# Blocked attention with a mixture of experts behind it: blank rows move to GpSimd's queue, the last batch's router tiles get a home of their own, and eight hand-written orders of steps are dealt anew

## The chip, the cores and the metric

The kernel runs on one core of a Trainium2 chip. TensorE (PE) multiplies, VectorE (DVE) and ScalarE (ACT) work elementwise, GpSimd (POOL) adds, computes powers and issues some DMAs, and SyncE (SP) issues the other loads. Each engine takes its instructions in the order in which they were written, and waits on semaphores for what other engines and DMAs owe it. The metric is the device time of one execution in microseconds (us), lower is better.

## The reference, cut to what matters

```python
# attention: 8 batches, 8 heads, 576 positions, 64 features, block-causal mask of 64
scores = np.where(mask, scale * q @ k.T, -1e9)
attn = np.exp(scores - scores.max(-1)); attn /= attn.sum(-1) + 1e-9
x = (attn @ v) with the heads side by side            # 4608 rows of 512
# router: cosine similarity to 8 experts, softmax, the best one alone
xn, en = x / (norm(x) + 1e-6), emb / (norm(emb) + 1e-6)
logits = xn @ en.T / tau
idx, gate_w = argmax(logits), softmax(logits)[idx]
# each row goes through its own expert: 512 -> 1024 -> 512
out[rows of e] = gate_w * (relu(x[rows of e] @ w1[e]) @ w2[e])
```

## The kernel before, in words

**Two halves.** The first half is attention and routing: 32 pairs of heads, numbered 0 to 31, four for each of the eight batches. The second half runs the experts over slots of 128 rows. Between them lies a handover, in which the last batch is routed while the first expert's weights are split and two early slots are worked.

**A pair in attention.** Instructions are written by a loop over the pairs (line 659). Each pair advances several generators, one step for each letter of a string in `PLANS` (line 22). `PLANS[0]` to `PLANS[3]` serve the four pairs of a batch, `PLANS[4]` to `PLANS[7]` those of pairs 28 to 31, and pair 0 has `PLAN0`. The letters are:

- `s`: the scores of pair n in five chunks. Each chunk is matmuls on PE into a two-bank PSUM buffer (`psp`, three of them) and an exponential on ACT into `pT`. After the third, the fourth and the fifth, POOL adds parts of `pT` into `pS` (line 347). These additions are called add 1 (after the third chunk), add 2 (the fourth), adds 3 and 4 (the fifth).
- `v`: the values of pair n-1 into the one PSUM tile `psb`. The first six steps are matmuls with V, the seventh the sums over keys (lines 392 to 397), which read `pT` and the finished `pS`, the eighth the copy `so` on ACT (line 399), the ninth is empty.
- `f`: finishing pair n-1. Two steps of small matmuls that read `so` and write `psb` again, then DVE's division into the row buffer (`xrow` or `xodd`, line 428), then the logits `lgh` (line 431).
- `m`: the row maxima of pair n+1, four steps of PE into `psp` and DVE out of it, one for the diagonal, one that transposes them.
- `p`: preparing pair n+2: transposes on PE into `psp`, `hi` on ACT, `lo` on DVE, two times.
- `l` and `w`: loads on SP's queue for pair n+3.
- `r`: one step of the router for the batch that ended before (`route`, from line 447).

What a pair has not done when its string ends is done at once.

**The router's steps.** The last pair of a batch is finished in the first pair of the next batch, and the router of the batch starts in the pair after that: its four router pairs are those numbered 4b+5 to 4b+8. It has 42 steps: 1 to 7 find the best expert on DVE, 8 ranks the rows with six small matmuls on PE, 9 and 10 add up the counts, 12 to 16 are five squares on ACT, 17 a power on POOL, 18 to 20 the places of the rows, 21 to 27 the gate (24 an exponential on ACT, 23 a product on DVE). Steps 30, 33, 36, 39 and 42 are `rows_out` (line 546), an indirect DMA issued by POOL that sends 128 rows to their places in the array `xs` in DRAM. They are called OUT 0 to OUT 4. For the seventh batch there are four more steps behind step 11, the squares are 16 to 20, the power 21, and the OUTs 32 to 36 follow without gaps; then two early slots are read back from `xs` (line 570).

In the strings before, the order of the other letters is the same in all eight. The `r` stand between them as follows, for a batch's four router pairs: steps 1 and 2, steps 3 to 13, steps 14 to 40, steps 41 and 42. In the third, OUT 0 stands before the third chunk of scores, OUT 1 between the third and the fourth, OUT 2 between the fourth and the fifth, OUT 3 behind it. For the seventh batch steps 1 to 31 are in pair 29, the five OUTs at the head of pair 30.

**Blank rows.** `blank(e)` (line 553) writes 128 rows of zeros (twice for expert 0) into `xs`, where an expert's first slot may read rows that nobody sends. It runs at the head of pairs 1, 2 and 3, for experts 0 to 2, 3 to 5, 6 and 7, and its nine DMAs are issued by SP.

**The handover's memory.** Attention's buffers lie in pools stacked from the right end of the memory: `st` outermost, then `xlast` (holding `xodd`), `xpool`, `rt`, `sm` (the router's small tiles, two of each, and a scratch) and `ptp`. When the chain of the last batch's routing is written, these pools but `st` are given up, and `ring(1)` puts the second layer's split weights over them: `ring_h1`, 32 KB in each partition, and `ring_l1`, 32 KB. A new tile waits for all instructions and DMAs that still use an old tile under it. The first to write is ACT (line 711, called by `seconds_in`, line 1123), and the piece stands ahead of the second half of `h` for early slot b (line 1094) in ACT's queue.

Of the kernel before, what the change touches and what calls it, by code (L numbers as in the profile page):

```python
# [8 lines left out]
F32 = mybir.dt.float32  # L9
F32R = mybir.dt.float32r  # L10
BF16 = mybir.dt.bfloat16
I32 = mybir.dt.int32
# [6 lines left out]


PLANS = (
    "vrvrrmrrmrmrrvrrvrrvrvrrvrrlrrvrsrrsrrprrmrfrrprrmrsrrfrrwrrvrsrrprrfrrsrfrrprrmrr",
    "vvmmmvvvvvlvssprmfpmsfwvspfsfpmr",
    "vvmrmmvrvvvrvlrvssrpmfrpmsrfwrvsprfsfrpmr",
    "vvrmrmrmrvrvrvrvrvrlvrsrsrprmrfrprmrsrfwrvrsrprfrsrfrprmr",
    "vrvrrmrmrrmrrvrvrrvrvrrvrrlrvrrsrsrrprrmrfrrprmrrsrrfrwrrvrsrrprrfrsrrfrprrmrr",
    "vrvrmrmrmrvrvrvrvrvrlrvrsrsrprmrfrprmrsrfrwrvrsrprfrsrfrprmrr",
    "vvrmrmrmvrvrvrvvrlrvrssrprmrfrpmrsrfrwvrsrprfsrfrprmr",
    "vrvrmrrmrmrvrrvrvrvrrvrlrrvrsrsrrprmrfrrprmrsrrfrwrrvrsrprrfrsrfrrprmrr",
)  # L30
PLAN0 = "mksmsmskmpkppmslpswp"

# [2 lines left out]
def kernel(  # L35
# [12 lines left out]
    nc = tc.nc  # L48
    B, H, S, D = q.shape
    E, DM, DF = w1.shape  # L50
    NT = B * S
    P = 128
    NP = H // 2
    NJ = (S - 64) // P + 1
# [17 lines left out]
    xs = dram.tile([E * RE * P, RW], F32, name="xs")  # L72
# [27 lines left out]
    ebase = iota("ebase", [P, NJ, E], [[0, NJ], [RE * P, E]])  # L100
# [54 lines left out]
    sm = pool(right, "sm", 2, side="right")  # L155
# [11 lines left out]
    def one_bank():  # L167
        return two_banks()[:, 0]
# [275 lines left out]
    def bc(ap, *shape):  # L444
        return ap.to_broadcast(shape)

    def route(b, xrow, lgh, ssp):

        lg = sm.tile([P, NJ, E], F32, name="lg")
        mx = sm.tile([P, NJ], F32, name="mx")  # L450
        t1 = sm.tile([P, NJ, E], F32, name="t1")
        ohb = sm.tile([P, NJ, E], BF16, name="ohb")
        nc.vector.tensor_reduce(lg, lgh.rearrange("p j h e -> p j e h"), axis=AX.X, op=ALU.add)
        yield
        nc.vector.tensor_reduce(mx, lg, axis=AX.X, op=ALU.max)
        yield
        nc.vector.tensor_tensor(lg, lg, bc(mx.unsqueeze(2), P, NJ, E), op=ALU.subtract)
        yield

        nc.vector.scalar_tensor_tensor(t1, lg, 0.0, erev, op0=ALU.is_ge, op1=ALU.mult)  # L460
        yield
        nc.vector.tensor_reduce(mx, t1, axis=AX.X, op=ALU.max)
        yield
        nc.vector.tensor_tensor(ohb, t1, bc(mx.unsqueeze(2), P, NJ, E), op=ALU.is_equal)
        yield
        nc.vector.memset(ohb[0:64, 0, :], 0.0)
        yield

        rk_ps = one_bank() if b < B - 1 else ps_m.tile([P, 512], F32, name="psm")
        rk = rk_ps[:, 0:NJ * E].rearrange("p (j e) -> p j e", e=E)  # L470
        yield "pe"
        nc.tensor.matmul(rk, triS, ohb, start=True, stop=False)
        for j in range(NJ - 1):
            nj = NJ - 1 - j
            nc.tensor.matmul(rk[:, j + 1:NJ, :], onesb, bc(ohb[:, j:j + 1, :], P, nj, E), start=False, stop=False)
        nc.tensor.matmul(rk, onesb, bc(acc.unsqueeze(1), P, NJ, E), start=False, stop=True)
        if b < B - 1:
            t2 = above(rk, ebase)
        else:
            ends.append((rk, ohb))  # L480
        yield
        oa = sm.tile([P, E], F32, name="oa")
        nc.vector.tensor_reduce(oa, ohb.rearrange("p j e -> p e j"), axis=AX.X, op=ALU.add)
        yield
        nc.vector.tensor_tensor(acc, acc, oa, op=ALU.add)
        yield
        if b == B - 1:
            nc.vector.tensor_tensor(accb, acc, early, op=ALU.subtract)
        yield "counted"
        if b == B - 2:  # L490

            c0 = one_bank()[:, 0:1]
            nc.tensor.matmul(c0, onesb, acc[:, 0:1], start=True, stop=True)
            lack = sm.tile([P, 1], F32, name="lack")
            yield
            nc.vector.scalar_tensor_tensor(lack, c0, -1.0, lim, op0=ALU.mult, op1=ALU.add)
            yield
            nc.vector.tensor_scalar(lack, lack, 0.0, float(EARLY), op0=ALU.max, op1=ALU.min)
            yield
            nc.vector.tensor_tensor(acc[:, 0:1], acc[:, 0:1], lack, op=ALU.add)  # L500
            yield

        ss = sm.tile([P, NJ], F32, name="ss")
        gs = sm.tile([P, NJ], F32, name="gs")
        if b < B - 1:
            for j in range(NJ):
                squares(xrow[:, j, 0:DM], ss[:, j:j + 1])
                yield
        else:
            nc.vector.tensor_reduce(ss, ssp, axis=AX.X, op=ALU.add)  # L510
        nc.gpsimd.tensor_tensor(ss, ss, half, op=ALU.pow)
        yield
        if b < B - 1:
            rowj = yield from places(t2, ohb)
        nc.vector.tensor_scalar(ss, ss, 1.0e-6, None, op0=ALU.add)
        yield
        nc.vector.reciprocal(ss, ss)
        yield
        nc.vector.tensor_tensor(lg, lg, bc(ss.unsqueeze(2), P, NJ, E), op=ALU.mult)
        yield  # L520
        nc.scalar.activation(lg, lg, AF.Exp)
        yield
        nc.vector.tensor_reduce(gs, lg, axis=AX.X, op=ALU.add)
        yield
        nc.vector.tensor_scalar(gs, gs, 1.0e-9, None, op0=ALU.add)
        yield
        if b == B - 1:
# [25 lines left out]
    def blank(e):  # L553

        t = ex[0]
        if e == 0:
            nc.gpsimd.memset(t, 0.0)
            nc.gpsimd.memset(t[:, DM + 1:DM + 2].bitcast(I32), 1 << 30)
        for r in range(EARLY if e == 0 else 1):
            r0 = (e * RE + r) * P  # L560
            nc.sync.dma_start(xs[r0:r0 + P, :], t)

    def token(tail):
        return tail[:, 1:2].bitcast(I32)
# [5 lines left out]
            nc.gpsimd.dma_start(ex[u], xs[u * P:(u + 1) * P, :])  # L570
            yield

    def above(rk, base):
        t = sm.tile([P, NJ, E], F32, name="t2")
        nc.vector.tensor_tensor(t, rk, base, op=ALU.add)
        return t

    def places(t, ohb):

        row = sm.tile([P, NJ], F32, name="row")  # L580
        rowj = sm.tile([P, NJ], I32, name="rowj")
        nc.vector.tensor_tensor(t, t, ohb, op=ALU.mult)
        yield
        nc.vector.tensor_reduce(row, t, axis=AX.X, op=ALU.add)
        yield
        nc.vector.tensor_tensor(rowj, row, drop, op=ALU.add)
        yield
        return rowj
# [70 lines left out]
    for n in range(NPAIR):  # L659
        pTs = pTf[n % 2]  # L660
        parts = {"s": scores(n, pTs), "v": pv, "f": post(n - 1) if n >= 1 else None,
                 "m": maxes(n + 1) if n + 1 < NPAIR else None,
                 "p": prep(n + 2) if n + 2 < NPAIR else None}
        for e in range(3 * n - 3, min(3 * n, E)) if n else ():
            blank(e)
        for c in PLANS[n % NP + (NP if n >= NPAIR - NP else 0)] if n else PLAN0:
            if c == "w":
                if n + 3 < NPAIR:
                    load_v(n + 3)
            elif c == "l":  # L670
# [326 lines left out]
    def chain():  # L997
# [13 lines left out]
            yield c  # L1011

        rk, ohb = ends[0]
        pg = places(above(rk, ebase), ohb)
        next(pg)
        next(rg)
        next(pg)
# [2 lines left out]
        rowj = finished(pg)  # L1020
# [17 lines left out]
    mx = ctx.enter_context(tc.tile_pool(name="mx", bufs=1, reuse_waits="tile"))  # L1038
# [64 lines left out]
    a, b = ea  # L1103
# [190 lines left out]
```

## Time and profile before

| what | value |
|---|---|
| median of 3 runs | 878.1 us (876.48 to 878.93) |
| the profiled execution | 880.13 us |
| its span, first to last instruction | 878.5 us |
| PE busy | 813.9 us, 93% |
| DVE busy | 530.1 us, 60% |
| POOL busy | 415.6 us, 47% |
| ACT busy | 404.6 us, 46% |
| mean granted clock of TensorE | 0.972 of full speed |

The profiled execution lies 2.0 us over the median, and 1.6 us of it lie around its span. Busy time of PE is modelled and matmuls overlap, so 93% says that PE is nearly always at work, and the idle rest is what a change of order can win. In the rows below a pair is cut from one copy `so` to the next, so that a stretch holds the second half of one string and the first of the next.

### The profile page before, as it was taken

The page shows a single profiled execution, that of the slowest core. Times are in us where ns is not written, and L with a number is a line of the kernel's source. Part 1 is how long each engine was busy: PE and PEld are TensorE (multiplying, and loading weights), DVE is VectorE, ACT ScalarE, POOL GpSimd, SP SyncE. Part 2 cuts the span into 40 slices and gives each one's busy share as a digit, 9 for nine tenths or more (in the row PEclk, how much of TensorE's full clock was granted, in tenths as well). Part 3 has the DMA queues.
Part 4 walks back from the last instruction along what each step waited for, and adds up shares of the span by engine and source line. Part 5 has one row for each costly group of instructions (what it writes and reads, how often), then busy time and mean ns, then how long its engine had stood idle before and what let it go on. Part 6 is the DMA issues. An engine that isn't in the chain of part 4 may idle for free. (4 is left out here: it accounts for less than half of the span.)

```text
span 878.5 us, 21354 instructions
## 1 busy us (share of the span) xinstructions
PE 813.9 (93%) x6569; PEld 643.9 (73%) x6569; DVE 530.1 (60%) x992; ACT 404.6 (46%) x733; POOL 415.6 (47%) x547
## 2 busy tenths in 40 slices
PE   6899989898999989858969999999999999999996
PEld 3677767676767767646657888888888888888875
DVE  5667767676775767652855534655767444666441
ACT  2344635545464546443634444654555333444321
POOL 4344564647464565644241133324455646465551
PEclk9899999999998999978989999999999999999998
DMA  4864444545345444507355453566687545354441
GB/s 72 185 148 83 74 109 82 138 83 122 79 91 109 84 118 73 126 1 244 125 198 196 159 167 96 175 213 220 219 259 230 183 137 160 108 182 156 137 134 40
DMA packets 147525, 121.17 MB, mean 138 GB/s; under 512 B 122991, under 2 KB 123311, under 8 KB 145837
## 3 DMA queue, kind: packets, MB, share of 16 engines
q1 hardware_dynamic: 123760, 64.50, 30.5%
q0 software_dynamic: 16976, 42.81, 16.4%
q10 hardware_dynamic: 6636, 12.09, 3.8%
q8 instruction: 63, 1.03, 0.5%
q14 instruction: 90, 0.73, 0.3%
HBM read 84.90 MB, written 35.27 MB: 137 GB/s over the span
## 5 line engine op out<-in xcount | busy, mean ns | idle before, releaser
L316 DVE TENSOR_REDUCE nmx<-psp 128x2 f32<-128x1024 f32 (+3 forms) x128 | 103.3, 824 | 85.3 <-PE psp L235 84.1
L365 ACT ACTIVATE pT<-psp 128x576 f32<-128x576 f32 (+2 forms) x192 | 112.4, 618 | 65.2 <-PE psp L235 51.1
L347 POOL TENSOR_TENSOR pS<-pT 128x896 f32<-128x896 f32 (+1 forms) x32 | 66.2, 2069 | 156.6 <-ACT pT L365 156.6
L235 PE MATMUL psp<-hi 64*128 64x448 f32 (+6 forms) x768 | 123.7, 354 | 9.0 <-ACT pT L365 4.0
L933 PE MATMUL py<-ring_h,hh 128*128 (+1 forms) x288 | 112.7, 391 | 0.5 <-issue 0.5
L933 PE MATMUL py<-ring_h,hl 128*128 (+1 forms) x288 | 112.2, 390 | 0.0
L933 PE MATMUL py<-ring_l,hh 128*128 (+1 forms) x288 | 112.1, 389 | 0.0
L933 PE MATMUL ph<-ring_h,xh 128*128 x280 | 110.1, 393 | 0.3 <-issue 0.3
L235 PEld LDWEIGHTS psp<-hi 64*128 64x128 f32 (+1 forms) x768 | 73.3, 190 | 48.9 <-DVE lo L301 16.0
L933 PE MATMUL ph<-ring_h,xl 128*128 x280 | 109.1, 389 | 0.0
L933 PE MATMUL ph<-ring_l,xh 128*128 x280 | 109.0, 389 | 0.0
L383 PE MATMUL psb<-pT,vo 128*64 128x448 f32 (+4 forms) x768 | 101.9, 401 | 6.6 <-DVE lgh L431 5.4
L347 POOL TENSOR_TENSOR pS<-pS,pT 128x640 f32<-128x640 f32 (+3 forms) x96 | 95.4, 994 | 8.0 <-ACT pT L365 1.4
L891 POOL DMA_DIRECT2D hq<-hrows x92 | 50.3, 553 | 101.1 <-DVE px L861 85.0
L715 DVE TENSOR_TENSOR ring_l<-raw,ring_h 128x1024 f32 (+1 forms) x64 | 77.6, 1224 | 22.7 <-ACT ring_h L711 13.7
L399 ACT COPY so<-psb 128x896 f32<-128x896 f32 x32 | 29.1, 909 | 129.4 <-PE psb L397 115.7
L951 ACT ACTIVATE h<-ph 128x512 f32<-128x512 f32 x70 | 41.7, 598 | 83.2 <-PE ph L933 70.7
L383 PEld LDWEIGHTS psb<-pT,vo 128*64 128x64 f32 x768 | 47.9, 138 | 42.1 <-issue 22.8
L711 ACT CAST ring_h<-raw 128x1024 f32 (+1 forms) x64 | 66.5, 1053 | 14.6 <-DMA xs<-xodd,rowj 8.4
L235 PE MATMUL psp<-qa,ka 64*128 64x288 f32 (+4 forms) x384 | 61.6, 302 | 1.8 <-DMA qa<-nmT 1.8
L933 PEld LDWEIGHTS py<-ring_h,hh 128*128 128x128 f32 x288 | 54.1, 188 | 12.0 <-issue 0.9
L933 PEld LDWEIGHTS py<-ring_h,hl 128*128 128x128 f32 x288 | 54.1, 188 | 11.3
(240 smaller groups left out, 1666.5 us busy)
## 6 DMA issues: line engine op xcount, KB each, us to landing
raw<-in_moe_w_dram SPq DMA_DIRECT2D x40, 512.0 KB
raw<-in_moe_w_dram SPq DMA_DIRECT2D x12, 1024.0 KB
hrows<-h ACTq DMA_DIRECT2D x46, 256.0 KB
hq<-hrows POOLq DMA_DIRECT2D x92, 128.0 KB
nat<-in_q_dram SPq DMA_DIRECT2D x64, 144.0 KB
nat<-in_k_dram SPq DMA_DIRECT2D x64, 144.0 KB
vo<-in_v_dram SPq DMA_DIRECT2D x64, 128.0 KB
xg<-xs POOLq DMA_DIRECT2D x64, 64.0 KB
```

The source lines that it names most:

```text
L235: nc.tensor.matmul(out(hh), lhsT(hd[hh]), rhs(hd[hh]), start=start, stop=stop)
L316: nc.vector.tensor_reduce(m[:, :, u], mx[:, :, 0:P * u], axis=AX.X, op=ALU.max, negate=True)
L347: eng.tensor_tensor(o, pT[0:r, hs, P:S] if t == 1 else o, pT[0:r, hs, off[t]:off[t] + w], op=ALU.add)
L365: nc.scalar.activation(pT[0:r, :, o:o + c1 - c0], st[0:r, :, x:x + c1 - c0], AF.Exp, scale=scale)
L383: nc.tensor.matmul(ob[hh * D:(hh + 1) * D, c0:c1], a[:, t, hh, :], pTs[0][:, hh, o:o + c1 - c0], start=(t == 0), stop=(c0 == OB or t == NJ ...
L399: nc.scalar.copy(so[n % 2][:, Q0:], ob[:, Q0:OB + S])
L711: return nc.scalar.copy(piece(ring_h, to, c, half), raw[i][:, c * CW:(c + 1) * CW])
L715: return eng.tensor_tensor(piece(ring_l, to, c, half), raw[i][:, c * CW:(c + 1) * CW], piece(ring_h, to, c, half).bitcast(F32), op=ALU.sub ...
L891: nc.gpsimd.dma_start(hq[32 * q_:32 * q_ + 32].rearrange("j (g x) -> j g x", g=GQ), rows[:, q_ % 2 * w:(q_ % 2 + 1) * w].rearrange("(g j) ...
L933: m = nc.tensor.matmul(out, a[:, c, :], w, start=(c == 0 and w is wh and a is sh), stop=(c == nk - 1 and a is sl_))
L951: nc.scalar.activation(h[:, f:f + 512], ph, AF.Relu)
```

## The change

Three edits:

1. `blank` issues its DMAs from POOL, and runs for experts 0 and 1 at the head of pair 2, for 2 and 3 at pair 3, for 4 and 5 at pair 4, for 6 and 7 at pair 5.
2. The small tiles of the last batch's router come from `st`, which is never given up, and no longer from `sm`: ten tiles, 768 bytes in each partition.
3. All eight strings are new. Besides the `r`, the other letters change places, and differently in each string. The `r` of a batch are now 11, 12, 10 and (of 15) 9: steps 1 to 11, 12 to 23, 24 to 33, 34 to 42. OUT 0 stands before the first chunk of scores of the third pair, OUT 1 behind the last, OUT 2 to OUT 4 in the next pair before its second chunk. For the seventh batch steps 1 to 35 are in pair 29, the power ahead of the third chunk of scores.

```diff
 PLANS = (
-    "vrvrrmrrmrmrrvrrvrrvrvrrvrrlrrvrsrrsrrprrmrfrrprrmrsrrfrrwrrvrsrrprrfrrsrfrrprrmrr",
-    "vvmmmvvvvvlvssprmfpmsfwvspfsfpmr",
-    "vvmrmmvrvvvrvlrvssrpmfrpmsrfwrvsprfsfrpmr",
-    "vvrmrmrmrvrvrvrvrvrlvrsrsrprmrfrprmrsrfwrvrsrprfrsrfrprmr",
-    "vrvrrmrmrrmrrvrvrrvrvrrvrrlrvrrsrsrrprrmrfrrprmrrsrrfrwrrvrsrrprrfrsrrfrprrmrr",
-    "vrvrmrmrmrvrvrvrvrvrlrvrsrsrprmrfrprmrsrfrwrvrsrprfrsrfrprmrr",
-    "vvrmrmrmvrvrvrvvrlrvrssrprmrfrpmrsrfrwvrsprfsrfrprmr",
-    "vrvrmrrmrmrvrrvrvrvrrvrlrrvrsrsrrprmrfrrprmrsrrfrwrrvrsrprrfrsrfrrprmrr",
+    "vrvmrrmmvvvrrrlvvvrmsrrsprfrpsmrrfsrpswfrfpmv",
+    "vrvmmmvrvvrvvvmrsrpfspsrmrfslfsrfprmrrpwv",
+    "vrvmmmvrvrvrrrvvmlvsrsrprfprsmrffsfsrvpwpm",
+    "vvmrrmmvvvrvrvmvrlprrsrfprssmvfspfsfrmwp",
+    "vrrrvlmrmrrmrvvrrvrrvrvvrrwmrrrsrrrspfrpsmrrfrrrspsrvffrmrp",
+    "vvrrmrmrvrvvrrmlrvvrrmrrrrvrrprprsrrfrsrsrmrfrsprfpfrrrmsrrrrvrwr",
+    "vvvrmmmrvrvvlvrmvrspfrpssmrfrfprsfmswrpv",
+    "vlmmvvvrvvrmrmrvvspsfrsfpwpfssvfpmmr",
 )
...
+    def small(b):
+        return sm if b < B - 1 else st
+
     def route(b, xrow, lgh, ssp):
 
-        lg = sm.tile([P, NJ, E], F32, name="lg")
...
+        lg = small(b).tile([P, NJ, E], F32, name="lg")
...
         for r in range(EARLY if e == 0 else 1):
             r0 = (e * RE + r) * P
-            nc.sync.dma_start(xs[r0:r0 + P, :], t)
+            nc.gpsimd.dma_start(xs[r0:r0 + P, :], t)
...
+    def places(b, t, ohb):
+
+        row = small(b).tile([P, NJ], F32, name="row")
+        rowj = small(b).tile([P, NJ], I32, name="rowj")
...
-        for e in range(3 * n - 3, min(3 * n, E)) if n else ():
+        for e in range(2 * n - 4, min(2 * n - 2, E)) if n > 1 else ():
             blank(e)
```

The same replacement is made for `mx`, `t1`, `ohb`, `oa`, `ss`, `gs` and `t2`.

## Rows read from the trace of the kernel before

**Rows 1.** Windows: length, busy time (and instructions) of PE, PEld, DVE, ACT, POOL; clock, DMA.
```profile
49.87:61.12 11.25, 10.98 (x143) 8.37 (x145) 8.11 (x18) 5.36 (x11) 5.11 (x4) 1.00 0.73 163
95.20:106.81 11.61, 11.33 (x149) 8.46 (x149) 8.66 (x23) 8.76 (x20) 5.88 (x5) 1.00 0.42 68
155.67:169.18 13.51, 11.09 (x143) 8.32 (x145) 9.26 (x26) 5.47 (x11) 9.19 (x9) 1.00 0.68 150
169.18:181.08 11.90, 10.96 (x143) 8.35 (x145) 7.75 (x17) 5.56 (x11) 6.73 (x8) 1.00 0.36 93
265.74:279.48 13.74, 13.47 (x143) 11.04 (x145) 7.23 (x15) 5.56 (x11) 6.72 (x8) 0.75 0.32 76
83.94:364.12 280.18, 258.79 (x3281) 196.10 (x3281) 197.93 (x482) 145.27 (x296) 154.79 (x137) 0.98 0.49 100
379.10:401.49 22.39, 14.94 (x159) 11.36 (x159) 10.85 (x28) 10.89 (x32) 11.16 (x10) 0.77 0.24 72
364.12:424.14 60.02, 46.63 (x524) 36.21 (x525) 29.58 (x74) 31.26 (x72) 27.44 (x28) 0.86 0.36 116
520.00:878.50 358.50, 351.21 (x1583) 291.26 (x1581) 194.52 (x211) 150.49 (x230) 172.46 (x280) 0.99 0.54 166
```

**Rows 2.** Waits of PE: who for whom, us in total, times, longest.
```profile
PE psb L393 <- POOL pS L347: 17.3, 19, 2.4
...
PE psb L383 <- DVE lgh L431: 5.4, 2, 5.3
...
PE psp L472 <- DVE ohb L466: 3.2, 1, 3.2
```

**Rows 3.** Timeline of POOL in a third router pair: start, us, what, [idle before].
```profile
160.72 2.10 POOL L347 TENSOR_TENSOR pS<-pT 128x896 f32<-128x896 f32 x1 [0.71 <-ACT pT L365]
162.99 0.99 POOL L546 DMA_INDIRECT xs<-xodd,rowj  x1 [0.17 <-issue]
164.01 1.56 POOL L347 TENSOR_TENSOR pS<-pS,pT 128x640 f32<-128x640 f32 x1
165.74 1.00 POOL L546 DMA_INDIRECT xs<-xodd,rowj  x1 [0.16 <-issue]
166.76 1.54 POOL L347 TENSOR_TENSOR pS<-pS,pT 128x384 f32<-128x384 f32 x2
...
174.80 2.10 POOL L347 TENSOR_TENSOR pS<-pT 128x896 f32<-128x896 f32 x1 [3.94 <-ACT pT L365]
```

**Rows 4.** Timeline of PE: two waits of that boundary, and one for `so`.
```profile
168.35 0.46 PE L393 MATMUL psb<-pS,ones 128*32 128x320 f32 x1 [2.28 <-POOL pS L347]
...
171.41 0.36 PE L235 MATMUL psp<-hi 64*128 64x192 f32 x2 [0.76 <-ACT pT L365]
...
402.45 0.45 PE L235 MATMUL psb<-idx,so 64*128 64x72 f32 x4 [2.10 <-ACT so L399]
```

**Rows 5.** Router instructions of DVE: ns least, median, most; first and last start.
```profile
L457 DVE TENSOR_TENSOR lg<-lg,mx x8: 190/190/917, 92.7 to 431.2; 128x40 f32<-128x40 f32 x8
...
L515 DVE TENSOR_SCALAR ss<-ss x8: 164/165/1505, 107.5 to 435.4; 128x5 f32<-128x5 f32 x8
```

**Rows 6.** Timeline of ACT: a square of the seventh batch, and the handover's first piece.
```profile
382.38 0.64 ACT L442 ACTIVATE xs<-xrow 128x512 f32<-128x512 f32 x1
...
446.24 1.04 ACT L711 CAST ring_h<-raw 128x1024 fp32r<-128x1024 f32 x1 [8.44 <-DMA xs<-xodd,rowj]
```

**Rows 7.** Timeline of DVE at the handover.
```profile
440.79 1.27 DVE L973 TENSOR_TENSOR hl<-pe,hh 128x512 fp32r<-128x512 f32 x2
447.31 1.23 DVE L715 TENSOR_TENSOR ring_l<-raw,ring_h 128x1024 fp32r<-128x1024 f32 x1 [5.25 <-ACT ring_h L711]
```

**Rows 8.** Timeline of PE at the handover.
```profile
447.83 1.97 PE L964 MATMUL pe<-ident,h 128*128 128x128 f32 x8 [8.67 <-ACT h L1094]
...
450.02 0.63 PE L933 MATMUL pss<-ring_l,hh 128*128 128x512 f32 x1
```

**Rows 9.** POOL's issue of a direct DMA of one blank's size: ns least, median, most.
```profile
L570 POOL DMA_DIRECT2D ex<-xs x2: 578/606/633, 408.9 to 409.6; - x2
```

More of the change, by code (lines that the diff above doesn't have):

```diff
@@ L21 @@
 PLANS = (
-    "vrvrrmrrmrmrrvrrvrrvrvrrvrrlrrvrsrrsrrprrmrfrrprrmrsrrfrrwrrvrsrrprrfrrsrfrrprrmrr",
-    "vvmmmvvvvvlvssprmfpmsfwvspfsfpmr",
-    "vvmrmmvrvvvrvlrvssrpmfrpmsrfwrvsprfsfrpmr",
-    "vvrmrmrmrvrvrvrvrvrlvrsrsrprmrfrprmrsrfwrvrsrprfrsrfrprmr",
-    "vrvrrmrmrrmrrvrvrrvrvrrvrrlrvrrsrsrrprrmrfrrprmrrsrrfrwrrvrsrrprrfrsrrfrprrmrr",
-    "vrvrmrmrmrvrvrvrvrvrlrvrsrsrprmrfrprmrsrfrwrvrsrprfrsrfrprmrr",
-    "vvrmrmrmvrvrvrvvrlrvrssrprmrfrpmrsrfrwvrsrprfsrfrprmr",
-    "vrvrmrrmrmrvrrvrvrvrrvrlrrvrsrsrrprmrfrrprmrsrrfrwrrvrsrprrfrsrfrrprmrr",
+    "vrvmrrmmvvvrrrlvvvrmsrrsprfrpsmrrfsrpswfrfpmv",
[6 more added lines that the diff above has]
+    "vlmmvvvrvvrmrmrvvspsfrsfpwpfssvfpmmr",
 )
@@ L445, in bc @@
         return ap.to_broadcast(shape)
+    def small(b):
+        return sm if b < B - 1 else st
     def route(b, xrow, lgh, ssp):
-        lg = sm.tile([P, NJ, E], F32, name="lg")
-        mx = sm.tile([P, NJ], F32, name="mx")
-        t1 = sm.tile([P, NJ, E], F32, name="t1")
-        ohb = sm.tile([P, NJ, E], BF16, name="ohb")
+        lg = small(b).tile([P, NJ, E], F32, name="lg")
+        mx = small(b).tile([P, NJ], F32, name="mx")
+        t1 = small(b).tile([P, NJ, E], F32, name="t1")
+        ohb = small(b).tile([P, NJ, E], BF16, name="ohb")
         nc.vector.tensor_reduce(lg, lgh.rearrange("p j h e -> p j e h"), axis=AX.X, op=ALU.add)
@@ L477, in route @@
         if b < B - 1:
-            t2 = above(rk, ebase)
+            t2 = above(b, rk, ebase)
         else:
@@ L481, in route @@
         yield
-        oa = sm.tile([P, E], F32, name="oa")
+        oa = small(b).tile([P, E], F32, name="oa")
         nc.vector.tensor_reduce(oa, ohb.rearrange("p j e -> p e j"), axis=AX.X, op=ALU.add)
@@ L501, in route @@
             yield
-        ss = sm.tile([P, NJ], F32, name="ss")
-        gs = sm.tile([P, NJ], F32, name="gs")
+        ss = small(b).tile([P, NJ], F32, name="ss")
+        gs = small(b).tile([P, NJ], F32, name="gs")
         if b < B - 1:
@@ L513, in route @@
         if b < B - 1:
-            rowj = yield from places(t2, ohb)
+            rowj = yield from places(b, t2, ohb)
         nc.vector.tensor_scalar(ss, ss, 1.0e-6, None, op0=ALU.add)
@@ L571, in early_rows, with above @@
             yield
-    def above(rk, base):
-        t = sm.tile([P, NJ, E], F32, name="t2")
+    def above(b, rk, base):
+        t = small(b).tile([P, NJ, E], F32, name="t2")
         nc.vector.tensor_tensor(t, rk, base, op=ALU.add)
         return t
-    def places(t, ohb):
-        row = sm.tile([P, NJ], F32, name="row")
-        rowj = sm.tile([P, NJ], I32, name="rowj")
+    def places(b, t, ohb):
+        row = small(b).tile([P, NJ], F32, name="row")
+        rowj = small(b).tile([P, NJ], I32, name="rowj")
         nc.vector.tensor_tensor(t, t, ohb, op=ALU.mult)
@@ L1013, in chain @@
         rk, ohb = ends[0]
-        pg = places(above(rk, ebase), ohb)
+        pg = places(B - 1, above(B - 1, rk, ebase), ohb)
         next(pg)
```

## The prediction

> **What bounds the kernel now.** I read the windows first, pair by pair and then by stage [rows 1]. In a pair without router work PE is busy for 10.98 of 11.25 us, and from 520 us to the end for 351.21 of 358.50 us at a clock of 0.99. So PE sets the pace in both halves, and a change of order can win only where PE stands still or its clock is low. There are three such places.
>
> First, the boundary between batches. The pair that holds a batch's OUTs takes 13.51 us and the next 11.90 us, against 11.25 us. The list of waits has PE waiting for POOL's `pS` 17.3 us in all, up to 2.4 us at a time [rows 2]. POOL's timeline shows why [rows 3]: OUT 1 lies between add 1 and add 2 and OUT 2 between add 2 and adds 3 and 4, and each pushes the next add back by about 1.2 us (from the end of add 1 at 162.82 to 164.01 us). Add 4 ends at 168.30 us, and PE starts the sums that read it at 168.35 us, after 2.28 us of waiting [rows 4]. A second wait of 0.76 us follows for a PSUM buffer that ACT frees late, as ACT could not copy `so` before the sums.
>
> Second, the last four pairs. From the copy of pair 27 to that of pair 31 there pass 60.02 us at a clock of 0.86, and 22.39 us of them lie between two neighbouring copies, at 0.77 [rows 1]. PE waits 3.2 us for the one-hot rows `ohb` and 5.3 us for `lgh` there [rows 2], and 2.10 us for `so` [rows 4].
>
> Third, the handover. ACT's first piece of `ring_h1` waits 8.44 us for a DMA named `xs<-xodd,rowj` [rows 6], the second `h` stands behind it, and PE waits 8.67 us for that `h` [rows 8].
>
> **Part by part.** The sum is made against the profiled execution's 880.1 us.
>
> *OUTs out of the adds.* From 83.94 to 364.12 us there are 23 pairs in 280.18 us [rows 1]. At 11.25 us each, and 0.36 us more (11.61 less 11.25) for each of the six batches' ranks, they would take 260.9 us. So 19.3 us are lost at six boundaries, 2.9 us at a regular one; one lost more, as the clock fell after the wait (13.74 us at 0.75 in place of 11.90). In the new third string no OUT lies between the third chunk of scores and the end: OUT 0 is ahead of the first chunk, OUT 1 behind adds 3 and 4. OUT 2 to OUT 4 come in the next pair ahead of its add 1. Four OUTs in a row are about 4 x 1.3 = 5.2 us (0.99 us and a gap of 0.2 to 0.3), and POOL's free stretch from add 4 (168.30) to the next add 1 (174.80) is 6.5 us, so they fit; if they did not, add 1 would slip by what is over, and PE's sums with it. I take the whole 19.3 us off, bounded by 14 (if the OUTs overrun by 0.9 us a batch) and 22 (if the short waits for `pS` that other pairs have go too, as the diagonal's maxima now stand behind the third chunk and so give POOL a little more time).
>
> *Router steps under the adds.* Here is what the new order puts in their place. The steps on DVE whose two inputs both lie in SBUF mostly ran when POOL was not adding. Twice one ran under an add, and was held: `L457` took 917 ns where 190 is the median, `L515` 1505 ns where 165 is [rows 5], so 0.7 and 1.3 us were lost. The new first router string puts step 10 (the count) behind the fifth chunk, and the new second string puts step 23 (the product) there, both under adds 1 to 4, with the second `lo` queued behind them on DVE; the next pair's second maxima wait for that `lo` to free its PSUM buffer. The least is 0. The most is a hold by the longest add, 2.10 us [rows 3], all of it on PE, 2 x 6 x 2.1 = 25 us. The two holds seen average 1.0 us, and about half should be covered, as PE has the first 1.1 us of values and the first maxima in front of the second. I take 12 x 0.5 = 6 us. The rule behind this is in the Trainium skill, "SBUF — State Buffer", section "Who interferes with whom": a VectorE instruction with two SBUF inputs contends with a GpSimd instruction that reads SBUF, and the loser is fully blocked until the other ends. Both rows agree with it. By the rule at its full length the term would be the 25 us, a rival below.
>
> *The last four pairs.* Four pairs at 11.25 and one rank at 0.36 are 45.4 us, so 14.7 of 60.02 us are excess. In pair 29 the power on POOL stood behind add 1, DVE's next step waited for it and was then held under an add (the 1505 ns), and behind it in DVE's queue stood the division and `lgh`, which PE awaits before the next values. Now the power is ahead of the third chunk, so ahead of add 1. What is new: steps 1 to 8 are packed into the head of pair 29, so the wait for `ohb` stays at about half, 1.6 us. All five squares stand between the copy `so` and the second chunk's exponential on ACT, 5 x 0.64 = 3.2 us [rows 6]; ACT has idle time there, but the exponentials free PE's buffers, so I charge 3.2 us. The five OUTs of the seventh batch take about 5 x 1.3 = 6.5 us ahead of pair 30's add 1, in a stretch of about 6.5 us less what adds 3 and 4 of pair 29 take longer; I charge 0.9 us. That leaves 5.7 of 14.7 us, so 9 us are won. Bounds: 14 (all gone and the clock full) and 3 (`lgh` alone goes, and its clock loss stays).
>
> *The home of the last router tiles.* By the sizes of the tiles, stacked from the right, `ring_h1` lies over all of `sm`, so over `rowj`, which the five OUTs of the last batch read; `xodd` lies beyond the end of `ring_l1`. With `rowj` in `st` nothing that the OUTs read lies under either (`xodd` moves 768 bytes down and stays clear of `ring_l1` by 64). ACT's piece can then run at 437.8 us (446.24 less 8.44), and PE's transposes of `h` soon after 439.2 us (447.83 less 8.67). What is late next is DVE: its two `hl` run until 442.06 us, then the first piece of `ring_l1` takes 1.23 us [rows 7] to 443.3 us. PE's first matmul with it began at 450.02 us [rows 8]; now at about 443.5, so 6.5 us are won. Bounds: 0 and 8.7 us. Router, places and OUTs themselves move by nothing.
>
> *Blank rows.* Nine issues by POOL cost about 0.6 us each [rows 9], two or three in a pair, 1.2 to 1.8 us behind add 4, in the 6.5 us in which POOL waits for the next add 1. The rows of the next OUTs come a pair later, in pair 7. So I take 0; if the cover were gone it would be 9 x 0.6 = 5.4 us. On SP's queue they cost nothing that shows: the pair from 49.87 to 61.12 us, into which some of them fall, takes 11.25 us like others [rows 1]. The same section of the Trainium skill warns that an issue from GpSimd's queue is starved while VectorE holds the port, from about 620 to 3100 ns in its example. By an estimate from that page two such issues would take 6.2 us and still about fit the free stretch, so the term would stay near 0; no row here shows a direct issue over 633 ns.
>
> The second half is full of PE work, so it starts earlier and ends earlier by the same.
>
> **The sum.** -19.3 + 6 - 9 - 6.5 + 0 = -28.8 us; 880.1 - 28.8 = 851.3 us. The profiled execution is 2.0 us over the median of the runs, so for the median I say 849 us.
>
> **Rivals.**
>
> 1. *The holds at full length.* DVE loses 25 and not 6 us: 849 + 19 = 868 us. For it: both rows of a hold. Against: the medians of both steps stand at their least, so a hold is the exception.
>
> 2. *The handover's wait stays*, as another tile under `ring_h1` is still in use, or the piece waits for its weights: 849 + 6.5 = 855.5 us. That edit would then not do what it says. Against: the releaser's name, and the sizes.
>
> 3. *Slower: every pair waits for `so`.* The new strings put fewer steps of PE between the sums and `f` (maxima, one chunk, transposes, where two chunks stood). If the copy then comes later than PE by x, all 29 pairs from 2 to 30 lose x, and from x = 1.0 us the gain of 29 us is gone. Where fewer steps stood between, in pair 30, PE waited 2.10 us for `so` [rows 4], though why ACT came late there the rows do not show. At 1.3 us a pair: 849 + 38 = 887 us.
>
> 4. *The second half gives it back*, as weights or rows come no earlier: half of the 29 us lost, 864 us. Against: PE is busy there for 98% of the time.
>
> **How the numbers follow.** Forecast 0.67, rival 1 0.12, rival 2 0.10, rival 3 0.06, rival 4 0.05. The range reaches from 836 us (the better ends of the second, third and fourth terms for the most part) to 866 us (rival 2 and rival 4 inside, rival 1 just outside); 0.18 is left out. A change of 0.3%, 2.6 us, is about what a measurement of this kernel can tell from none. Faster 0.92 (all but rival 3, and a little of the rest), within 0.3% 0.02, slower 0.06.
>
> **What would show it.** In the trace after: POOL's adds without an indirect DMA between add 1 and add 4; no wait of PE for `pS` over 1 us; boundaries of 11 to 12 us a pair; the first `ring_h1` without a wait for `xs<-xodd,rowj`, and PE's wait before the transposes under 2 us; the stretch from pair 27's copy to pair 31's near 51 us. I would be wrong by holds of `L485` and `L519` near 1 us or more, by waits of PE for `so` or for exponentials in each pair, by a low clock in the attention half, or by OUTs that overrun into add 1.

## The result, and the profile after

The changed kernel takes 836.7 us (median of 4 runs, 835.79 to 839.6) against 878.08 us before: a ratio of 0.954, interval 0.951 to 0.957. The forecast was 849 us, with a range of 836 to 866. Of the experiments below, runs 1 to 4 shared one chip, runs 5 to 8 a second and runs 9 to 12 a third, each time with the kernel before beside them. The gain came out the same on the first two (runs 3 and 7). On the third the same program took 878.3 us; the part on runs 9 to 12 is about that.

The profiled execution takes 839.6 us, its span is 837.9 us, so 40.5 us are gone against the 880.1 us of before. The windows of the kernel after; columns as in [rows 1]:

```profile
82.52:93.29 10.77, 10.77 (x149) 8.29 (x149) 8.99 (x25) 9.16 (x20) 5.75 (x8) 1.00 0.43 113
93.29:104.21 10.92, 10.69 (x143) 8.19 (x145) 9.16 (x24) 5.71 (x12) 6.11 (x5) 1.00 0.57 102
104.21:115.24 11.03, 10.84 (x145) 8.21 (x146) 8.33 (x20) 5.57 (x11) 6.83 (x6) 1.00 0.35 78
115.24:126.00 10.76, 10.73 (x145) 8.15 (x144) 8.38 (x18) 5.36 (x11) 8.65 (x10) 1.00 0.78 207
82.52:332.78 250.26, 247.72 (x3283) 189.06 (x3281) 200.61 (x482) 149.61 (x297) 152.96 (x138) 1.00 0.49 110
345.57:362.26 16.69, 14.45 (x144) 9.25 (x144) 10.42 (x28) 10.78 (x31) 8.86 (x8) 0.80 0.18 54
332.78:383.79 51.01, 44.68 (x524) 32.29 (x523) 30.39 (x76) 31.03 (x72) 29.36 (x30) 0.93 0.49 159
479.50:837.90 358.40, 351.41 (x1584) 291.53 (x1583) 194.49 (x211) 150.78 (x230) 172.67 (x280) 1.00 0.53 166
```

Cut at the same four places as [rows 1], the 40.5 us are these. Up to the copy of pair 4: 1.4 us (83.94 to 82.52). Pairs 4 to 27: 280.18 to 250.26, so 29.9 us. Pairs 27 to 31: 60.02 to 51.01, so 9.0 us. From there to the end: 454.36 to 454.11, so 0.25 us. The second half takes 358.40 us where it took 358.50.

The list of waits of PE, after, answers to [rows 2]:

```profile
PE pe L915 <- DMA xg<-xs: 4.8, 1, 4.8
PE pe L967 <- DVE hl L976: 2.4, 1, 2.4
...
PE psb L383 <- DVE lgh L431: 2.0, 7, 0.6
PE psp L475 <- DVE ohb L469: 1.7, 1, 1.7
...
PE psb L393 <- POOL pS L347: 0.7, 1, 0.7
...
PE psb L235 <- ACT so L399: 0.2, 1, 0.2
```

The wait for `pS` fell from 17.3 to 0.7 us, that for `lgh` from 5.4 to 2.0, that for `ohb` from 3.2 to 1.7. PE waits for `so` once, for 0.2 us. At the handover the wait for `h` [rows 8] is gone, and a new one of 4.8 us for the fetched rows `xg` stands in its place. POOL at the end of a batch, after, answers to [rows 3]:

```profile
108.98 2.09 POOL L347 TENSOR_TENSOR pS<-pT 128x896 f32<-128x896 f32 x1 [2.42 <-ACT pT L365]
111.15 3.15 POOL L347 TENSOR_TENSOR pS<-pS,pT 128x640 f32<-128x640 f32 x3
114.59 1.02 POOL L549 DMA_INDIRECT xs<-xrow,rowj  x1 [0.29 <-issue]
...
118.47 0.97 POOL L549 DMA_INDIRECT xs<-xrow,rowj  x1 [0.30 <-issue]
119.72 2.10 POOL L347 TENSOR_TENSOR pS<-pT 128x896 f32<-128x896 f32 x1 [0.27 <-ACT pT L365]
```

Adds 1 to 4 now follow each other, and OUT 1 to OUT 4 fill the stretch to the next add 1, which starts 0.28 us after the last of them and waited for ACT's `pT`, not for them.

### The profile page after: what moved, and what is told of

It reads as the page before. It is cut to its first block, busy times and chain, and to the rows that moved or that the text cites. A ratio compares the mean times of both kernels' runs of the same rounds, so it can differ in the third digit from the quotient of the medians.

```text
span 837.9 us, 21353 instructions
## 1 busy us (share of the span) xinstructions
PE 804.3 (96%) x6569; PEld 633.4 (76%) x6569; DVE 533.0 (64%) x992; ACT 409.2 (49%) x733; POOL 424.2 (51%) x556
## 5 line engine op out<-in xcount | busy, mean ns | idle before, releaser
L235 PE MATMUL psp<-hi 64*128 64x64 f32 (+6 forms) x768 | 117.3, 340 | 5.4 <-DVE nmx L316 1.7
L383 PE MATMUL psb<-pT,vo 128*64 128x448 f32 (+4 forms) x768 | 104.0, 407 | 3.2 <-DVE lgh L431 2.0
L718 DVE TENSOR_TENSOR ring_l<-raw,ring_h 128x1024 f32 (+1 forms) x64 | 77.5, 1222 | 17.3 <-ACT ring_h L714 9.3
L301 DVE TENSOR_TENSOR lo<-psp,hi 128x640 fp32r<-128x640 f32 x64 | 48.5, 758 | 36.1 <-ACT hi L299 32.1
L936 PEld LDWEIGHTS py<-ring_h,hl 128*128 128x128 f32 x288 | 54.1, 188 | 11.3
```

What stands on the lines that cost most here:

```text
L235: nc.tensor.matmul(out(hh), lhsT(hd[hh]), rhs(hd[hh]), start=start, stop=stop)
L301: nc.vector.tensor_tensor(lo_[i][:, :, cs], src, hi_[i][:, :, cs].bitcast(F32), op=ALU.subtract)
L383: nc.tensor.matmul(ob[hh * D:(hh + 1) * D, c0:c1], a[:, t, hh, :], pTs[0][:, hh, o:o + c1 - c0], start=(t == 0), stop=(c0 == OB or t == NJ ...
L718: return eng.tensor_tensor(piece(ring_l, to, c, half), raw[i][:, c * CW:(c + 1) * CW], piece(ring_h, to, c, half).bitcast(F32), op=ALU.sub ...
L936: m = nc.tensor.matmul(out, a[:, c, :], w, start=(c == 0 and w is wh and a is sh), stop=(c == nk - 1 and a is sl_))
```

## The experiments

### 1 to 3: each of the three edits alone

Run 1 keeps only the home of the last router tiles, run 2 only the blank rows on POOL's queue and in their new pairs, run 3 only the strings.

```diff
 # run 1, in all ten places
-        ss = sm.tile([P, NJ], F32, name="ss")
+        ss = small(b).tile([P, NJ], F32, name="ss")
 # run 2
-            nc.sync.dma_start(xs[r0:r0 + P, :], t)
+            nc.gpsimd.dma_start(xs[r0:r0 + P, :], t)
 # run 3: the eight strings of the change, nothing else
```

> The kernel before with the second edit alone (the last batch's ten small router tiles in st). Theory from the trace after: the wait of ring_h1 for the OUTs goes, but the ring_l1 pieces on DVE then run while POOL issues OUT 3, hold it for some 4.5 us, the rows land late, and the first slot's fetch makes PE wait about as long: 878 us, within 2 us of before. Rival (the prediction's step): the handover wins 6.5 us: 871.5 us.

> The kernel before with the first edit alone (blank rows issued by POOL in pairs 2 to 5). Theory: nothing or up to 1.5 us won, as the pairs 1 to 3 lose some traffic: 876.5 to 878. Rival: the issues hold POOL and the adds slip: 880 to 883 us.

> The kernel before with the eight new strings alone. Theory: nearly the whole gain, as the handover of the trace after gives back what the second edit takes: 837 to 839 us. Rival: the second edit is worth 6.5 us under the new strings too: 843 us.

Run 1: 876.36 us against 875.97, ratio 1.000 (0.998 to 1.002). Run 2: 876.75 us, ratio 1.000 (0.999 to 1.002). Run 3: 836.74 us, ratio 0.954 (0.953 to 0.956). So the strings carry the whole gain, and the two other edits neither cost nor win anything that shows. POOL and DVE at the handover of run 1, where `ring_h1` no longer waits for the OUTs:

```profile
439.02 5.54 POOL L549 DMA_INDIRECT xs<-xodd,rowj  x1 [0.30 <-issue]
444.86 0.97 POOL L549 DMA_INDIRECT xs<-xodd,rowj  x1 [0.30 <-issue]
452.73 0.60 POOL L852 DMA_DIRECT2D xg<-xs  x1 [6.90 <-issue]
```
```profile
439.10 4.61 DVE L718 TENSOR_TENSOR ring_l<-raw,ring_h 128x1024 fp32r<-128x1024 f32 x4
```

DVE's four pieces of `ring_l` start 0.08 us after OUT 3 has started, run for 4.61 us without a gap, and OUT 3, which takes 0.97 us elsewhere, takes 5.54. The rows of the OUTs land late, the slot's fetch isn't issued before 452.73 us, and PE waits for it (4.3 us in run 1). The wait for `h` was exchanged for a wait for `xg`.

### 4: only the OUTs out of the adds

The strings of before, with OUT 1 to OUT 3 of the third router pair moved behind the fifth chunk.

```diff
-    "vvrmrmrmrvrvrvrvrvrlvrsrsrprmrfrprmrsrfwrvrsrprfrsrfrprmr",
+    "vvrmrmrmrvrvrvrvrvrlvrsrsrprmrfrprmrsfwvspfsfprrrm",
```

> The kernel before with one string changed: in the third router pair of batches 0 to 5 no router step stands between OUT 0 and the end of the string but OUT 1 behind the fourth step of f; OUT 2 to OUT 4 fall to the head of the next pair. All other letters keep their order. Theory: the six boundaries' 19 us go and the pairs stay at 11.25 us: about 860 us. Rival: the boundary is bound otherwise and gives back half: 868 us. If all of the new strings' gain came from the OUTs it would be 846 us or less.

860.02 us, ratio 0.981 (0.979 to 0.983), so 16.0 us less than before. Three of its windows, the pair with the ranks, the one in which OUT 2 to OUT 4 now lie, and pairs 4 to 27:

```profile
91.94:103.57 11.63, 11.37 (x149) 8.49 (x149) 8.68 (x23) 8.76 (x21) 5.89 (x5) 1.00 0.40 69
114.84:126.02 11.18, 11.01 (x143) 8.39 (x145) 7.73 (x17) 5.36 (x11) 8.69 (x10) 1.00 0.66 178
80.68:341.60 260.92, 254.91 (x3281) 192.51 (x3281) 197.89 (x482) 144.23 (x297) 152.43 (x135) 1.00 0.50 104
```

The 23 pairs take 260.92 us: the 260.9 that the prediction reckoned from 11.25 us a pair, 19.3 less than in the profile of [rows 1]. On run 4's own chip less was there to win: with the old strings these pairs take 277.6 and 277.8 us in the traces of runs 1 and 2, so 16.8 us are gone. What is left of the gain in these pairs, 260.92 less 250.26, is 10.7 us, and it is in no term of the sum.

PE still waits for `pS` here, 20 times, nearly always for a fraction of a microsecond, and so do its weight loads (`PEld`). In the list of all waits of this run:

```profile
PEld psb L393 <- POOL pS L347: 15.9, 28, 4.2
...
PE psb L393 <- POOL pS L347: 7.8, 20, 3.9
```

### 5: and the diagonal's maxima behind the third chunk

In all eight strings of run 4 the diagonal's maxima (the fifth `m`) and the third chunk of scores (the third `s`) change places. It is one of the moves in the new strings, and it gives PE more to do between add 1's chunk and the sums.

```diff
-    "vvmrmmvrvvvrvlvrssrpmfrpmsrfwrvsprfsfrpmr",
+    "vvmrmmvrvvvrvlvrssrpmfrpsmrfwrvsprfsfrpmr",
```

> The kernel with the moved OUTs, and in all eight strings the diagonal's maxima and the third chunk of scores change places (the third chunk goes first). Theory: in the pairs before, the third chunk takes the PSUM buffer that DVE's first lo has just left and waits some 0.4 us for it; the maxima need it later and shorter. The sums' wait for POOL's add 4 (0.2 to 0.4 us a pair) shrinks too. So most of the difference between 11.25 and 10.75 us a pair comes from this swap: 860 less 28 x 0.4 = 849 us. Rival: the gain per pair lies in the other letters (the short maxima and f moved ahead): 857 to 860 us.

872.68 us against 877.79, ratio 0.995 (0.993 to 0.997): slower than run 4, where 849 was expected. The windows show a loss in the pairs with ranks and a gain in the others:

```profile
91.01:105.88 14.87, 12.46 (x149) 8.90 (x149) 12.05 (x29) 8.75 (x20) 6.28 (x5) 0.89 0.49 88
116.71:127.57 10.86, 10.79 (x143) 8.22 (x145) 7.81 (x18) 5.34 (x10) 8.67 (x10) 1.00 0.71 183
```

Ordinary pairs fell to 10.8 to 10.9 us, as expected, and the waits of PE for `pS` from 20 to 1. But five of the six pairs with ranks rose from 11.6 to 14.9 us, with a lower clock in part of them (0.89), and the sixth and the pair behind it to 13.3 and 13.1 us. POOL and DVE in the first of them:

```profile
96.04 2.09 POOL L347 TENSOR_TENSOR pS<-pT 128x896 f32<-128x896 f32 x1 [5.97 <-ACT pT L365]
```
```profile
96.05 2.11 DVE L485 TENSOR_TENSOR acc<-acc,oa 128x8 bf16<-128x8 bf16 x1
98.17 0.17 DVE L423 TENSOR_SCALAR rin<-psb 128x6 f32<-128x6 f32 x1
...
99.43 0.23 DVE L431 TENSOR_TENSOR lgh<-psb,rin 128x80 f32<-128x80 f32 x1
```

Step 10, `acc`, of 128x8 elements, took 2.11 us. In run 4 its eight instances took 166 to 170 ns. There the first ran at 96.78 us and add 1 started at 97.33; the exchange brings the third chunk forward, and add 1 with it, so that both start together. Behind `acc` in DVE's queue stand the division and `lgh`, for which PE then waits 2.41 us before the next values. It is the first rival of the prediction, the hold at full length, in a place where nothing covers it.

### 6: the OUTs back among the adds of the kernel after

```diff
-    "vvmrrmmvvvrvrvmvrlprrsrfprssmvfspfsfrmwp",
+    "vvmrrmmvvvrvrvmvrlprrsrfprssmvfrsrrpfrsfrmwp",
```

> The changed kernel with OUT 1 between the third router pair's third and fourth chunk and OUT 2 between its fourth and fifth, as before; the other letters stay. Theory: PE waits some 2.3 us for pS at each of six boundaries again, with a little slack from the new order: 836.7 + 6 x 2 = 849 us. Rival: the new order has enough slack to hide the OUTs, 838 us or less.

856.8 us (852.3 to 862.1), ratio 0.975 (0.970 to 0.980): 20 us slower than the kernel after. The pair with the OUTs and the next:

```profile
149.47:162.73 13.26, 10.98 (x145) 8.18 (x145) 8.51 (x20) 5.56 (x10) 8.81 (x8) 1.00 0.52 124
162.73:174.92 12.19, 12.16 (x145) 9.62 (x144) 8.19 (x17) 5.55 (x11) 6.67 (x8) 0.86 0.53 118
```

The wait for `pS` is back at 14.3 us, and the pair behind it loses by a lower clock too. With run 4, the place of the OUTs is worth 16 us in the old order and about 20 us in the new.

### 7 and 8: the handover, the pieces later or the weights later

In run 7 DVE's pieces wait for a small tile that POOL writes behind the last OUT. In run 8 the 2 MB of weights that SP loads meanwhile are issued later.

```diff
 # run 7
             rows_out(xrow, rowj, j)
+        nc.gpsimd.memset(past[:, 0:1], 0.0)
...
+    nc.vector.tensor_copy(past[:, 1:2], past[:, 0:1])
     seconds_in((0,))
 # run 8
-    load_raw(1, 1)
...
     ht_copy(b, 4, ptb[1])
+    load_raw(1, 1, eng=nc.scalar)
```

> The changed kernel, but DVE starts the second layer's lo pieces only when POOL has issued the last batch's five OUTs (one small tile written by POOL behind OUT 4 and copied by DVE ahead of the pieces). Theory: OUT 3 falls from 5.5 to 1.0 us, OUT 4 ends near 403 and not 407.5 us, its rows land by 406, the first slot's fetch is there in time and PE's wait of 4.8 us goes; the pieces come 2.2 us later: 836.7 - 2.6 = 834 us. Rival: OUT 3 is slow from the weights' transfer and not from DVE: OUT 3 stays near 5 us and the time is 838 to 839 us.

> The changed kernel, but the second expert's second-layer weights are requested by ACT after slot b's last hidden copy, some 8 us later than now, so that their 2 MB do not run beside the last batch's OUTs. Theory: OUT 3 still takes 5.5 us (DVE's pieces hold it), but OUT 4's rows land some 4 us earlier and the fetch with them: PE's wait falls from 4.8 to about 1 us, 833 us. Rival: OUT 3 falls to 1 us, so that the transfer was what held it; then 832 us. If the landing is not what delays the fetch, 836.7 us.

Run 7: 834.76 us (832.31 to 835.89), ratio 0.952 (0.948 to 0.956). Run 8: 835.81 us, ratio 0.952 (0.948 to 0.956). POOL in run 7:

```profile
397.04 0.98 POOL L549 DMA_INDIRECT xs<-xodd,rowj  x1 [0.30 <-issue]
...
401.91 0.59 POOL L852 DMA_DIRECT2D xg<-xs  x1 [2.50 <-DMA xs<-xodd,rowj]
```

With the pieces behind the OUTs, OUT 3 takes 0.98 us again and the wait for `xg` is gone; PE waits 2.43 us for the first piece of `ring_l` instead. In run 8 OUT 3 still takes 5.54 us and PE waits 4.1 us for `xg`. So it is DVE's pieces that hold OUT 3, not the transfer of the weights; that is shown. The fetch suffers from both. It is issued 18.2 us behind the start of OUT 0 in the kernel after, 13.5 in run 8 and 8.9 in run 7: the hold costs it 4.6 us, and the weights another 4.7, in which the rows of OUT 4 land late. Run 8 takes the second part away, but there PE starts on the fetched rows 7.6 us after the fetch's issue and not 3.7, so its wait hardly changes; that the weights, then issued beside the fetch, slow it is likely and not shown. What run 7 wins, at most 2 us, is near what can be told.

### 9 to 12: step 10 ahead of the third chunk; the kernel after again, on another chip

Run 9 is run 5 with steps 9 and 10 ahead of the third chunk. Run 10 is the kernel after itself, run 11 run 7 again, run 12 runs 7 and 8 together.

```diff
 # run 9, against run 5
-    "vvmrmmvrvvvrvlvrssrpmfrpsmrfwrvsprfsfrpmr",
+    "vvmrmmvrvvvrvlvrssrpmfrprrsmfwvsprfsfrpmr",
```

> The kernel before with OUT 1 to OUT 3 behind the fifth chunk and the diagonal's maxima exchanged with the third chunk of scores, as in the run that came to 872.7 us, but with router steps 9 and 10 now ahead of the third chunk in the second router string, so that no step of two inputs stands in front of the third step of f while add 1 runs. If the loss of 3.3 us at each rank pair was the hold of step 10 under add 1: step 10 back at 0.17 us, every rank pair near 11.2 us, other pairs at 10.8 to 10.9 us, and about 849 us (860 us less 0.35 us for each of 29 pairs). If the loss came from the exchange itself or from the ranks (PE's six small matmuls and what waits for them): rank pairs stay near 14.9 us and the time near 872 us.

> The changed kernel once more, for the comparison with the two next to it on one chip: 836 to 838 us, OUT 3 held for 5.5 us beside DVE's four pieces of the second ring.

> The changed kernel with DVE's four pieces of the second ring held back until POOL has issued the last batch's OUTs, in the same job as the changed kernel itself. If the pieces' hold on OUT 3 costs what the first look showed: 2 us under the changed kernel, about 835 us, with OUT 3 at 1 us and no wait of PE for the slot's rows. If the four pieces are what PE needs next anyway, so that only a wait changes its place: no difference.

> The changed kernel with both: DVE's four pieces behind the last OUT, and the 2 MB of weights on SP's queue issued by ACT only after the fourth copy of ht, so that the rows and the slot's fetch have the queues to themselves. If transfer time of rows and fetch is what is left behind the held issue: the fetch lands 1 to 2 us earlier than with the pieces alone and the time is 833 to 834 us. If the queues are not the limit: as with the pieces alone, 835 us, or slower by the later weights.

None of the times came out as expected: 882.26, 878.28, 879.10 and 879.51 us, with the kernel before at 881.89 us (median of 29 runs). The ratios are 0.999 (0.996 to 1.002), 0.996 (0.993 to 0.998) and 0.996 (0.993 to 0.999) for runs 9 to 11. The six times of run 12 lie between 865.4 and 882.2 us, too far apart for a verdict. So the program that won 41 us before won 3.6 us on this chip, and the kernel before took 4 to 6 us more there than in the other three series.

The windows of run 10 show where the time goes. The pair with a batch's ranks is not shown; these are the pair ahead of the OUTs and the one with them, to be set beside the third and fourth window of the kernel after, and the last such pair:

```profile
101.17:112.44 11.27, 11.09 (x147) 8.47 (x149) 8.51 (x21) 5.57 (x10) 7.10 (x6) 1.00 0.36 79
112.44:128.45 16.01, 13.78 (x143) 11.13 (x140) 7.86 (x16) 5.68 (x11) 8.40 (x10) 0.79 0.49 134
362.79:382.16 19.37, 16.25 (x149) 10.81 (x147) 11.07 (x26) 5.58 (x11) 8.59 (x10) 0.74 0.37 104
```

From the copy of pair 7 on, one pair in each batch takes 16.0, 19.0, 15.4, 16.7, 19.4 and 19.4 us where the kernel after takes 10.7 to 10.8 us (12.8 the last). These six hold 39.2 us, and the whole span is 36.3 us longer; the other pairs up to there take 10.7 to 11.3 us, as in the kernel after. POOL, PE and ACT in the first of the six:

```profile
114.15 0.98 POOL L549 DMA_INDIRECT xs<-xrow,rowj  x1 [0.30 <-issue]
115.43 0.98 POOL L549 DMA_INDIRECT xs<-xrow,rowj  x1 [0.30 <-issue]
120.60 2.09 POOL L347 TENSOR_TENSOR pS<-pT 128x896 f32<-128x896 f32 x1 [4.19 <-ACT pT L365]
```
```profile
116.18 0.65 ACT L365 ACTIVATE pT<-psp 128x576 f32<-128x576 f32 x1 [2.83 <-remote]
```
```profile
114.64 0.26 PE L418 MATMUL psb<-ident,so 33*128 33x33 f32 x2 [0.27 <-issue]
115.36 0.22 PE L235 MATMUL psb<-idx,so 64*128 64x72 f32 x1 [0.47 <-issue]
116.10 0.45 PE L235 MATMUL psb<-idx,so 64*128 64x72 f32 x3 [0.52 <-issue]
117.52 0.33 PE L418 MATMUL psb<-ident,so 33*128 33x33 f32 x2 [0.98 <-issue]
```

From the issue of OUT 3 (114.15 us) until 1.1 us behind that of OUT 4, PE goes on by a few small matmuls at a time, 0.7 us apart and then 1.4, and waits for nothing that the trace names. ACT's next exponential comes after 2.83 us for which the trace has only the word `remote`. After that the granted clock is at the lower of its two levels, 1.2 GHz, for part of the pair (0.79 of full speed in the mean). The OUTs themselves take 0.97 to 0.98 us, as elsewhere. Between the copies of pairs 0 and 31 of run 10, idle stretches of PE or ACT over 0.4 us without a named releaser stand in these six pairs and in pair 29, with the five OUTs of the seventh batch, and nowhere else; the kernel after has none there. In run 9, with another order of letters but the same four OUTs in a row, the pair with them takes 16.78 us; in run 5, with the same place for the OUTs on the earlier chip, 10.86 us. So in the traces kept the cost goes with the chip and with the row of OUTs together. What stands between them is open: no trace of the kernel before was taken on that chip, fewer OUTs in a row were not tried there, and as all runs on it came in one series, the chip can't be told apart from the occasion.

Run 9's own question its windows still answer, in the pair with the ranks:

```profile
90.76:102.01 11.25, 11.09 (x149) 8.44 (x149) 9.19 (x24) 8.75 (x21) 5.66 (x5) 1.00 0.41 70
112.97:129.75 16.78, 14.24 (x143) 9.78 (x143) 9.26 (x18) 5.72 (x10) 8.59 (x10) 0.80 0.57 143
```

That pair takes 11.25 us and no longer 14.87, and `acc` is back at 166 to 169 ns. So the hold of step 10 was what run 5 lost, and the exchange itself costs nothing. In the whole time of run 9 this can't be seen.

Runs 10 and 11, side by side on one chip, don't differ in time, and from the copy of pair 31 to the end they take 452.4 and 452.2 us. The 2 us of run 7 are thus not confirmed.

## Why the prediction was right, and where not

*OUTs out of the adds, -19.3 us.* Right in its mechanism: where it was tried alone (run 4) the 23 pairs end at the 260.9 us reckoned, with the waits and the boundaries as described, and run 6 confirms it from the other side. The size is some 3 us too large: on run 4's chip 16.0 us were won. The profile before had longer boundaries than the traces of that chip; the pair behind the OUTs takes 11.9 us and more in it, and 11.2 us in half of the cases in runs 1 and 2.

*Router steps under the adds, +6 us.* The steps are held, but less. `acc` is `L485` before and `L488` after, the product `L519` and `L522`:

```profile
L485 DVE TENSOR_TENSOR acc<-acc,oa x8: 166/168/170, 100.1 to 433.3; 128x8 bf16<-128x8 bf16 x8
```
```profile
L519 DVE TENSOR_TENSOR lg<-lg,ss x8: 199/201/202, 107.9 to 435.9; 128x40 f32<-128x40 f32 x8
```
```profile
L488 DVE TENSOR_TENSOR acc<-acc,oa x8: 167/434/439, 88.7 to 392.1; 128x8 bf16<-128x8 bf16 x8
```
```profile
L522 DVE TENSOR_TENSOR lg<-lg,ss x8: 200/743/1426, 99.4 to 394.6; 128x40 f32<-128x40 f32 x8
```

The medians lost 0.27 and 0.54 us, and the pairs that hold them take 10.77 and 10.92 us, the first two windows after, so next to nothing of it reaches PE. A hold is not the exception that the first rival's counter-argument made of it: in the first six batches both steps start 1.7 and 1.4 us into add 1, every time, and end 0.02 to 0.06 us behind its end. In the new strings both stand behind `f`, which makes them late and the hold short, and is what separates them from run 5. The Trainium skill's rule in "SBUF — State Buffer", section "Who interferes with whom", that the loser is blocked until the other ends, is what run 5 shows at its full length: 2.11 us beside an add of 2.09. One of the two rows that the prediction read as steps with two inputs in SBUF is none: `L515` is a `tensor_scalar` on `ss` alone [rows 5]. It was held all the same, for 1.50 us, so the rule of two inputs as the prediction gives it does not cover that row.

*What the sum lacked: 10.7 us.* The step that failed is the upper bound of the first term. It named a cause, that the short waits for `pS` in other pairs go too because the diagonal's maxima stand behind the third chunk, and sized it at 2.7 us at most. Four pairs of a batch took 45.3 us in run 4; with the exchange they take 10.94, 11.25, 10.83 and 10.87 us, so 43.9 us (the second, with the ranks, from run 9, the others from run 5), and 43.5 us in the kernel after. So the exchange is worth about 1.4 of 1.8 us a batch, 0.35 us in every pair; the rest, from other moves in the strings, was not taken apart. The reading that misled me was that PE is busy for 10.98 of 11.25 us and so can't gain. In the kernel after it is busy for 10.77 of 10.77. Over the 23 pairs PE's busy time fell from 254.91 us in run 4 to 247.72, and its idle time only from 6.0 to 2.5. So part of what counted as busy was waiting: a weight load that stands for `pS` can lie beside the modelled end of the matmul ahead of it, and then doesn't appear among PE's own waits. The list of waits of the weight loads, before and after, shows it:

```profile
PEld psb L393 <- POOL pS L347: 24.7, 26, 2.6
```
```profile
PEld psb L393 <- POOL pS L347: 2.5, 8, 1.0
```

In run 4 it is 15.9 us, 9.7 of them in the 23 pairs. In run 5 these 9.7 fell to 1.0, while the weight loads' waits there for DVE's `lo`, 12.0 and 12.2 us, stayed. So the exchange works through `pS`, as the term says, and not through the buffer that `lo` leaves, as was expected of run 5.

*The last four pairs, -9 us.* 51.01 us, as forecast, and `ohb` at 1.7 us for 1.6. In run 4, which keeps the old strings there, the stretch takes 60.3 us; the four new strings were not run by themselves. The agreement is partly luck: four pairs of a batch now take 43.5 and not 45.4 us, so the excess is 7.5 us where 5.7 were charged. Most of it lies in pair 28, 16.69 us at a clock of 0.80.

*The home of the last router tiles, -6.5 us.* This step failed: from the copy of pair 31 on 0.25 us are won in the kernel after, and nothing in run 1. The mechanism up to PE's transposes is right: ACT's piece runs at 396.41 us without a wait, and PE's transposes of `h` wait for DVE's `hl` alone, 2.43 us where it was 8.67 [rows 8] and under 2 was expected, and PE's first matmul with `ring_l` starts 6.0 us behind the start of OUT 0 where it was 12.7. I let "Router, places and OUTs themselves move by nothing" stand, and there it broke. DVE's pieces, which came behind the OUTs before because the wait held them there, now run beside OUT 3 and hold its issue for 4.6 us. The slot's fetch is late by that and by the weights (runs 7 and 8), and PE's wait of 4.8 us for `xg` takes back most of what was won. That DVE can hold an issue on POOL the prediction says of the blank rows; I did not carry it over to the handover. That OUT 3 is held because its issue reads row numbers from SBUF is likely, and not shown. The second rival had the time for it, 855.5 us from this term alone, but with another cause.

*Blank rows, 0.* Right (run 2). The 620 and 3100 ns that the prediction takes from the Trainium skill stand in "SBUF — State Buffer", section "A bandwidth-pool intuition that's wrong (but worth ruling out)", not in the section that it names. No run here shows such a hold of a direct issue.

*Rivals.* Rival 3 did not come about: 0.2 us for `so` in all. Nor did rival 4: the second half takes the same 358.4 us. Rival 1 is real as a mechanism (run 5), and the new strings avoid its price.

The errors have opposite signs: 10.7 and 6 us too little, 6.5 us too much. The sum without them, 849 - 16.7 + 6.3, gives 838.6 us; the 1.4 us ahead of pair 4 are most of the rest. That 836.7 us lies inside the range, by 0.7 us, is therefore luck in part: without the handover's loss of 6.3 us it would have fallen below it. On the chip of runs 9 to 12 the forecast does not hold: 878.3 us lies outside its range, and no rival described that.

## What to carry to other kernels

Where an engine reads as busy all the time, look at the waits of its weight loads and at whether equal stretches of work have equal lengths, before taking it for the bound. A wait that is taken away also released what queued behind it: list what starts earlier, and which slow instruction it will run beside. A gain from a denser order should be timed on more than one chip before it is relied on.

## What the runs showed of the hardware

- A POOL instruction that issues an indirect DMA was held by DVE's elementwise instructions with two SBUF inputs: 5.54 us for 0.98, in three kernels at the same place (the kernel after, runs 1 and 8), and 0.98 when DVE came later (run 7). The Trainium skill, "SBUF — State Buffer", section "Who interferes with whom", has DVE instructions with two SBUF inputs contend with a GpSimd instruction that reads SBUF, but tells of a probe in which `tensor_tensor` stalled no DMA, and infers why; here the trace shows that an indirect one is held. Its issue ended 0.85 us after the last of four such instructions, which followed each other without a gap (run 1).
- The other way round, a DVE instruction of 0.17 us took 2.11 us beside POOL's add of 2.09 (run 5), and 0.43 us where it started 1.7 us into the add (the kernel after).
- One program took 836.7 us on one occasion and 878.3 us on another chip, 5% more. In the traces the difference lies in the six pairs in which four indirect DMAs are issued in a row, where PE and ACT stall with no releaser named and the granted clock falls to 1.2 GHz behind it. Why is open.
